# Two layers of convolution and SwiGLU on one core: the same instructions, every engine's queue in a newly searched order

## The chip, the core and the metric

The kernel runs on one core of a Trainium2 chip. The metric is the device time of one execution in microseconds; the time of a kernel is the median of its runs. An execution that the hardware profiler followed gives a trace beside the times: every instruction with its engine, start, duration and what it waited for.

## The reference

`reference(q, k, v, shift_k, ssm_k, ssm_D, x, w_gate, w_up, w_down)` applies two identical layers to x = q, in bf16, with batch 1, S = 2048 rows, D = 512 columns and F = 1792 hidden columns:

```python
def _A_ref(q, k, v, shift_k, ssm_k, ssm_D):
    k_shift = sum over t of k_pad[:, t:t + S, :] * shift_k[:, ks - 1 - t]      # 4 taps, causal
    kv = k_shift * v
    y = irfft(rfft(kv, 2 * S) * rfft(ssm_k, 2 * S))[:, :S]                     # long causal convolution per column
    return q * (y + kv * ssm_D)

def _B_ref(x, w_gate, w_up, w_down):
    return (silu(x @ w_gate) * (x @ w_up)) @ w_down

for _ in range(2):
    x = x + _A_ref(_layernorm(x), A_k, A_v, A_shift_k, A_ssm_k, A_ssm_D)
    x = x + _B_ref(_layernorm(x), B_w_gate, B_w_up, B_w_down)
```

`_layernorm` takes mean and variance over the 512 columns. The convolution's y doesn't depend on x, so the same y serves both layers.

## The kernel before

**The convolution.** k, v and the filter are cut into 4 blocks. The four-tap shift is done on TensorE: `dg` holds diagonal matrices made from the taps (L1372 on ScalarE, L1376 on VectorE, some on GpSimd), and a matmul of `dg` with k, transposed to `kTb`, gives shifted k in PSUM. k is transposed by TensorE for the first block and by SP's transposing DMAs (L460) for the later ones. The transforms are matmuls with cosine and sine blocks of 128x128. The forward ones, `fwd`, are computed at the start in two halves: angles on VectorE (L1324, L1328), Sin on ScalarE (L1330), negations on VectorE (L1336). The inverse ones, `inv`, are two transposing DMAs of `fwd` on SP (L1382). H and G are spectra of the filter, X those of kv; `product` multiplies them on VectorE (t, then Z: L748, L752), `m` is a sum or difference of Z (L889), and the inverse matmuls (L895) give y in PSUM.

**The prologue of a unit.** Work goes by units (layer, c, h) of 256 rows: layer 0 or 1, column of four rows c = 0 to 3, half h. For each, `apply_norm` makes n = layernorm(x), `prologue` forms x += n*y (L1004 to L1009), takes the second layernorm to z, and transposes z to `zT`: by SP's transposing DMA (L994), or on TensorE for the first unit (L1022). Statistics come in two ways: `ln_stats` on VectorE (L914, L915), and `ln_stats_act` on ScalarE (sums L929, mean L931, squares L938, variance `ve` L942). Both end in `power` (L905), an exponentiation on GpSimd that gives `rstd`. `shift_of` (L953) multiplies it with the mean on VectorE for those n that ScalarE normalises (L959).

**The feed-forward part of a unit.** Hidden columns go in groups of 4, 4, 4 and 2 tiles of 128. `pf` are gate and up products (L416, with zT), `sg` is silu of the gate, `ht` or `hr` the other factor, and `pd` the down products (L1210). In groups that `by_rows` makes, the hidden values come with rows on the partitions, so SP transposes them: `sg<-hr` (L1132). Five units use a product of seven instead of eight matrix blocks (L1085).

**What sets the order.** The functions above don't issue anything; they register 1716 operations with a planner (`Plan.add`), each with its engine, its cost, what it reads and writes, and a function that emits it. `ORDER` has one number for each operation, its rank, and `Plan.order` sorts by it. `walk` then goes through the sorted list once and assigns ring slots (PSUM banks and shared SBUF buffers); `issue` emits the instructions in that list's order under a manual schedule, so that each engine's queue, and SP's DMA queue, has the operations in the table's order. An engine runs its queue strictly in order. Ahead of the first real matmuls stand 33 warm-up matmuls (L1495).

```python
def order(self, table):
    assert len(table) == len(self.ops)
    seq = [o for _, o in sorted(zip(table, self.ops), key=lambda x: x[0])]
```

`bst` is a buffer of six slots for the statistics of VectorE; two memsets on GpSimd (L1276, L1277) fill its constant columns.

Of the kernel before, what the change touches and what calls it, by code (L numbers as in the profile page):

```python
# [343 lines left out]
def kernel(  # L344
# [79 lines left out]
    bst = whole("bst", [P, BN_SLOTS, 9], F32)  # L424
# [484 lines left out]
    def ln_stats(c, rows, pw=PW):  # L909
        n = len(rows)  # L910
        mv = new("mv", "mv", [P, n, 2], F32, parts=n)
        for o, i in enumerate(rows):
            st = plan.buf("bn", "bnst", lambda slot: bst.t[:, slot])
# [615 lines left out]
```

## Time and profile before

| | |
|---|---|
| time, median of 3 runs | 339.26 us (339.04 to 339.29) |
| profiled execution, first to last instruction | 337.7 us |
| TensorE busy | 330.9 us, 98% |
| VectorE busy | 299.9 us, 89% |
| ScalarE busy | 262.8 us, 78% |
| GpSimd busy | 35.4 us, 10% |
| granted TensorE clock | 1.000 |
| moved by DMA | 31.59 MB |

In the views of the profile PE is TensorE, PEld its weight loads, DVE VectorE, ACT ScalarE, POOL GpSimd, and SPq the DMA queue that SP issues. A row of the chain has its start and its length in microseconds, the engine, what was made, the line, and how many instructions it groups. A row of the timeline has start, length, engine, line, operation, what was made from what, the tile shapes and the count; in brackets stand the idle time before it and what ended that. A row of the waits has the time waited in all, how often, and the longest. A row of the windows has the stretch, its length, busy times of PE, PEld, DVE, ACT and POOL with their counts, the granted clock, the share that the DMA engines were busy, and GB/s. A duration on PE includes the pipelining with its neighbours.

### The profile page before, as it was taken

The numbers are of one execution on the slowest core, as the hardware profiler recorded it, in microseconds if no ns is written. First come the engines' busy times: TensorE is split into PE (matmuls) and PEld (weight loads), VectorE is DVE, ScalarE is ACT, GpSimd is POOL, SyncE is SP. The second block draws the span as 40 slices with busy tenths as digits, with TensorE's granted clock in tenths as the row PEclk, the third lists the DMA queues.
The fourth block names the chain that finished last, engine by engine and source line by source line (L and its number), as shares of the span: only waits on it lengthen the run. The fifth ranks groups of instructions, "written<-read, shape, count | busy, mean of one in ns | idle before, by whom it ended". The sixth has DMA issues, their size and how long they took to land.

```text
span 337.7 us, 5898 instructions
## 1 busy us (share of the span) xinstructions
PE 330.9 (98%) x2141; PEld 204.6 (61%) x2172; DVE 299.9 (89%) x512; ACT 262.8 (78%) x534; POOL 35.4 (10%) x48
## 2 busy tenths in 40 slices
PE   9999999999999999999999999999999999999996
PEld 7655864645445564745454464744455687858884
DVE  8899999999888998999999999999999787877545
ACT  7889999999967466999899894999675556475462
POOL 4050001102100000122010100011100100100000
PEclk9999999999999999999999999999999999999999
DMA  7999604632346147421324434510514230204101
GB/s 255 350 229 376 130 13 66 151 82 41 71 93 94 36 91 188 95 49 32 62 53 106 97 60 110 138 35 16 96 28 82 56 72 17 48 18 93 49 3 62
DMA packets 77993, 31.59 MB, mean 94 GB/s; under 512 B 69766, under 2 KB 75787, under 8 KB 77963
## 3 DMA queue, kind: packets, MB, share of 16 engines
q1 hardware_dynamic: 77808, 31.13, 39.6%
q8 instruction: 17, 0.28, 0.4%
q14 instruction: 14, 0.11, 0.1%
q10 hardware_dynamic: 154, 0.07, 0.1%
HBM read 12.33 MB, written 2.10 MB: 43 GB/s over the span
## 4 chain that ended last, share of the span: by engine, by line
PE 91%; ACT 4%; DMA 2%; issue 1%; DVE 1%; SPq 1%
PE pf L416 56%; PE pd L1210 20%; PE ps L1085 7%; PE ps L416 6%; DMA kTb<-in_A_k_dram 1%; PE wm L1495 1%; DMA sg<-hr 1%; ACT H L525 1%; SPq L1132 1%; ACT ks L620 1%; ACT n L959 0%; ACT jk L929 0%; DVE t L748 0%; ACT ev L525 0%; ACT hr L1124 0%
## 5 line engine op out<-in xcount | busy, mean ns | idle before, releaser
L416 PEld LDWEIGHTS <-zT 128*128 128x128 bf16 x528 | 51.6, 98 | 58.5 <-DMA zT<-z 0.2
L416 PE MATMUL pf<-wg_sb,zT 128*128 128x512 bf16 x255 | 64.3, 379 | 0.5
L416 PE MATMUL pf<-wu_sb,zT 128*128 128x512 bf16 x260 | 64.3, 379 | 0.2
L1210 PE MATMUL pd<-wd_sb,sg 128*128 128x512 bf16 x189 | 48.1, 379 | 0.9 <-DMA sg<-hr 0.3
L1124 ACT CAST hr<-pf 128x512 bf16<-128x512 f32 x66 | 38.4, 593 | 12.4 <-PE pf L416 8.5
L1123 ACT ACTIVATE sg<-pf 128x512 bf16<-128x512 f32 x66 | 38.8, 608 | 11.3 <-PE pf L416 10.2
L416 PE MATMUL pf<-zT,wg_sb 128*128 128x256 bf16 x368 | 46.0, 273 | 0.1
L416 PE MATMUL pf<-zT,wu_sb 128*128 128x256 bf16 x368 | 45.9, 273 | 0.0
L758 DVE TENSOR_TENSOR t<-X,G 128x4096 bf16<-128x4096 bf16 x18 | 40.9, 2284 | 0.1
L416 PEld LDWEIGHTS <-wu_sb 128*128 128x128 bf16 x368 | 36.0, 98 | 8.1
L416 PEld LDWEIGHTS <-wg_sb 128*128 128x128 bf16 x368 | 35.9, 98 | 7.9 <-issue 0.4
L1183 ACT ACTIVATE sg<-pf 128x512 bf16<-128x512 f32 x46 | 27.3, 607 | 10.8 <-PE pf L416 10.8
L1187 ACT CAST ht<-pf 128x512 bf16<-128x512 f32 x46 | 26.8, 595 | 9.8 <-PE pf L416 8.0
L905 POOL TENSOR_TENSOR rstd<-mv,nhalf 128x2 f32<-128x2 f32 x20 | 17.0, 852 | 158.2 <-DVE mv L915 134.7
L1210 PEld LDWEIGHTS <-sg 128*128 128x128 bf16 x200 | 19.5, 98 | 21.7 <-DMA sg<-hr 0.8
L1210 PE MATMUL pd<-wd_sb,ht 128*128 128x512 bf16 (+1 forms) x124 | 29.7, 369 | 0.1
L914 DVE BATCH_NORM_STATS2 bst<-xc 128x6 f32<-128x512 bf16 x40 | 26.5, 683 | 0.5
L905 POOL TENSOR_TENSOR rstd<-ve,nhalf 128x2 f32<-128x2 f32 x12 | 14.6, 1218 | 111.7 <-ACT ve L942 111.7
L1190 DVE TENSOR_TENSOR ht<-ht,sg 128x512 bf16<-128x512 bf16 (+1 forms) x31 | 16.6, 544 | 8.8 <-ACT sg L1183 4.5
L1130 DVE TENSOR_TENSOR hr<-hr,sg 128x1024 bf16<-128x1024 bf16 x27 | 18.4, 682 | 4.2 <-ACT sg L1123 2.0
L1210 PEld LDWEIGHTS <-ht 128*128 128x128 bf16 x126 | 12.3, 98 | 13.1 <-DVE ht L1190 0.3
L525 ACT ACTIVATE X<-ps 128x512 bf16<-128x512 f32 x32 | 18.4, 604 | 1.6 <-PE ps L416 0.9
(143 smaller groups left out, 522.1 us busy)
## 6 DMA issues: line engine op xcount, KB each, us to landing
hn<-in_A_ssm_k_dram SPq DMA_DIRECT2D x4, 512.0 KB, 3.7
vt<-in_A_v_dram SPq DMA_DIRECT2D x4, 512.0 KB, 5.5
xc<-in_A_q_dram SPq DMA_DIRECT2D x4, 512.0 KB, 5.6
out_dram<-xc SPq DMA_DIRECT2D x15, 128.0 KB, 1.9
wg_sb<-in_B_w_gate_dram SPq DMA_DIRECT2D x1, 1792.0 KB
wu_sb<-in_B_w_up_dram SPq DMA_DIRECT2D x1, 1792.0 KB, 8.9
wd_sb<-in_B_w_down_dram SPq DMA_DIRECT2D x1, 1280.0 KB, 12.1
sg<-hr SPq DMA_TRANSPOSE x66, 2.4
```

What stands on the lines that cost most here:

```text
L416: nc.tensor.matmul(o, lhsT=lhsT, rhs=rhs, start=(n == 0), stop=(n == len(terms) - 1))
L525: add("ACT", act(D), lambda: nc.scalar.activation(out=view(), in_=ps.t[:], func=ACT.Copy, scale=scale), r=[ps], w=[(buf, keys)], conv=conv)
L758: dve(8 * D, lambda t=t, part=part: nc.vector.tensor_mul(out=t.t[:], in0=x.t[:, :, part:part + 1, :].to_broadcast((P, R, 2, D)), in1=g.t[: ...
L905: add("POOL", cost, lambda: nc.gpsimd.tensor_tensor(out=rstd.t[:], in0=var(), in1=nhalf.t[:].to_broadcast((P, n)), op=ALU.pow), r=reads + ...
L914: add("DVE", 0.6, lambda st=st, i=i: nc.vector.bn_stats(out=st.t[:, 0:6], in_=xs[c].t[:, i, :]), r=[(xs[c], (i,))], w=[st])
L1085: nc.tensor.matmul(bank.t[:, half_ * C:(half_ + 1) * C], lhsT=lhsT(i), rhs=rhs(i), start=(first and i == 0 and half_ == 0), stop=(last and ...
L1123: add("ACT", act(D), lambda ps=ps, dst=dst, o=o, which=which: nc.scalar.activation(out=rows(dst, o), in_=ps.t[:], func=ACT.Silu) if which ...
L1124: out=rows(dst, o), in_=ps.t[:], func=ACT.Silu) if which == "g" else nc.scalar.copy(out=rows(dst, o), in_=ps.t[:]),
L1130: dve(n * W, lambda: nc.vector.tensor_mul(out=hr.t[:], in0=hr.t[:], in1=sg.t[:]), [sg], [hr], due=(unit, k / pairs, 0.0, "h"))
L1183: add("ACT", act(D), lambda ps=ps, o=o, sg=sg: nc.scalar.activation(out=sg.t[:, o:o + 2, :], in_=ps.t[:], func=ACT.Silu), r=[ps], w=[(sg, ...
L1187: add("ACT", act(D), lambda ps=ps, o=o, ht=ht: nc.scalar.copy(out=ht.t[:, o:o + 2, :], in_=ps.t[:]), r=[ps], w=[(ht, (o // 2,))], due=(uni ...
L1210: nc.tensor.matmul((pds[o] if not cs.start else pds[HP]).t[:, cs], lhsT=ht.tiles(q, o), rhs=wt["d"].t[:, ft, cs], start=(ft == std0 and no ...
```

## The change

`ORDER` is replaced as a whole: all 1716 ranks are new, and come from a new search in which the mean completion times of three engines are part of the objective. In the new order the first use of a statistics slot comes ahead of the memsets that create `bst`, so a small helper creates the buffer on first use. Nothing else differs; the built programs have the same instructions, and the order differs in the queues of TensorE, VectorE, ScalarE, GpSimd and SP. Behind the table the changed kernel's lines are two further down, and behind the helper seven.

```diff
 ORDER = [
-    7, 79, 141, 188, 2, 3, 1, 15, 23, 4, 12, 0, 5, 13, 68, 9, 10, 6, 8, 11, 28, 19, 14, 24, 20, 25, 32, 33, 38, 69, 144, 146, 18, 46, 17, 45, 22, 43,
...
-    1663, 1678, 1691, 1693, 1699, 1703, 1708, 1711, 1712, 1713, 1714, 1710, 1715,
+    3, 110, 0, 119, 4, 2, 1, 16, 15, 5, 6, 23, 24, 29, 30, 9, 8, 10, 7, 11, 25, 12, 39, 13, 14, 41, 43, 53, 56, 33, 34, 35, 31, 54, 32, 52, 28,
...
+    1670, 1643, 1646, 1639, 1656, 1683, 1698, 1707, 1681, 1682, 1650, 1659, 1699, 1700, 1708, 1709, 1710, 1711, 1712, 1713, 1714, 1715,
 ]
...
+    def stat_slot(slot):
+        if bst.t is None:
+            bst.t = bst.make(0)
+        return bst.t[:, slot]
+
     def ln_stats(c, rows, pw=PW):
...
-            st = plan.buf("bn", "bnst", lambda slot: bst.t[:, slot])
+            st = plan.buf("bn", "bnst", stat_slot)
```

What moves where, of the operations that the prediction speaks of: on ScalarE the second square L938 and the variance L942 of the first unit go ahead of two evictions of X, two L1372 and one copy of transposed filter rows go ahead of the second Sin, and the two L959 go ahead of several evictions of H. On VectorE the first unit's L953 goes from behind all products of the first block to behind the first product of its second half, and the two copies of the taps go ahead of the second half of the angles. On TensorE one inverse matmul goes ahead of the first matmul that reads the k transposed by DMA; the gate and up products are permuted within their groups. On SP the order is the same up to the up weights; behind them the two parts of the down weights change places, and later a load of v and a load of the filter go behind two transposes of hidden values.

126 rows, old and new, of the table ORDER are left out of this document.

## The prediction

> **What bounds the kernel now.** I read the page first, then the waits of TensorE, then the chain of work that ended last, and only then the timeline of the first 33 us and of one wait in layer 1.
>
> ```profile
> span 337.7 us, 5898 instructions
> PE 330.9 (98%) x2141; PEld 204.6 (61%) x2172; DVE 299.9 (89%) x512; ACT 262.8 (78%) x534; POOL 35.4 (10%) x48
> PEclk9999999999999999999999999999999999999999
> PE 91%; ACT 4%; DMA 2%; issue 1%; DVE 1%; SPq 1%
> sg<-hr SPq DMA_TRANSPOSE x66, 2.4
> ```
> ```profile
> PE ps L416 <- DMA kTb<-in_A_k_dram: 0.8, 1, 0.8
> ...
> PE pd L1210 <- DMA sg<-hr: 0.3, 1, 0.3
> PE ps L416 <- ACT ks L620: 0.2, 1, 0.2
> ```
> ```profile
> 4.78 1.00 PE pt L583 x16
> 5.78 0.89 PE pt L472 x16
> ...
> 125.07 5.18 PE pd L1210 x24
> ...
> 268.97 3.49 PE pf L416 x32
> ...
> 333.35 1.32 PE pd L1210 x12
> ```
>
> TensorE is busy 98% of the span at the full clock in every slice, and the chain is TensorE for 91%. So I ask how much of its time is not work. The chain prices a matmul: 5.18/24 = 0.2158 us for 512 columns, 3.49/32 = 0.1091 for 256, 0.89/16 = 0.0556 for 128. Counted from the program, which has the same matmuls before and after, there are 978 of 512 columns, 973 of 256, and 217 of 128, 33 of them warm-up that ends at 4.78; four tiny ones make the 2172 that the page's weight loads count. The work after the warm-up is 978 x 0.2158 + 973 x 0.1091 + 184 x 0.0556 = 211.1 + 106.1 + 10.2 = 327.4 us. It starts at 4.78, and the last matmul ends at 333.35 + 1.32 = 334.67: 329.9 us. **Only 2.5 us are waiting.** Another order of the same instructions can gain no more than that, because neither the warm-up nor the last 3 us change: the last 14 operations on TensorE (of the planner's 1716) stand in the same order in both kernels. How much it can lose has no such bound.
>
> The waits name three places, all in the rows above and below: 0.8 us for the k transpose at 22.76, 0.2 us and some issue gaps between 31.27 and 32.88, and 0.3 us at 241.33. Following the chain's starts against the summed work (its steps at these prices) I read them as about 1.0, 0.7 and 0.5 us, which makes up 2.2 of the 2.5.
>
> The profiled execution has a span of 337.7 us against a median of 339.26 for the runs. The 1.56 us between them lie outside the first and last instruction, and I carry them over unchanged: predicted change of the span = predicted change of the time. What a measurement of this kernel can tell from no change is about 0.2%, or 0.68 us.
>
> **The change part by part: the start-up.** Until the first gate/up matmul at 32.88 both orders have the same 84 TensorE steps, so this stretch ends where its longest chain ends. These rows carry it:
>
> ```profile
> 4.54 13.09 SPq L1382 DMA_TRANSPOSE inv<-fwd  x2
> 17.68 2.68 SPq L460 DMA_TRANSPOSE kTb<-in_A_k_dram  x1
> ...
> 29.30 7.83 SPq L460 DMA_TRANSPOSE kTb<-in_A_k_dram  x1
> ```
> ```profile
> L1382 SPq DMA_TRANSPOSE inv<-fwd x2: 5288/6491/7694, 4.5 to 12.3; - x2
> ```
> ```profile
> 3.89 0.63 ACT L1330 ACTIVATE fwd<-ph 128x512 bf16<-128x512 int32 x1 [0.26 <-DVE ph L1328]
> 4.42 0.68 ACT L1372 ACTIVATE dg<-ident,tapF 128x128 bf16<-128x128 bf16 x2
> ```
> ```profile
> 15.64 1.28 DVE L748 TENSOR_TENSOR t<-X,G 128x1024 bf16<-128x1024 bf16 x2
> 16.33 0.60 ACT L525 ACTIVATE X<-ps 128x512 bf16<-128x512 f32 x1 [0.26 <-PE ps L564]
> ...
> 17.69 0.71 ACT L938 ACTIVATE jk<-xc,nm 128x512 bf16<-128x512 bf16 x1
> ...
> 19.76 0.31 ACT L942 ACTIVATE ve<-sm,eps 128x2 f32<-128x2 f32 x1
> ...
> 20.11 0.68 DVE L889 TENSOR_TENSOR m<-Z 128x1024 bf16<-128x1024 bf16 x1
> 20.15 4.36 POOL L905 TENSOR_TENSOR rstd<-ve,nhalf 128x2 f32<-128x2 f32 x1 [13.43 <-ACT ve L942]
> ...
> 22.76 1.08 PE L416 MATMUL ps<-dg,kTb 128*128 128x128 bf16 x16 [0.82 <-DMA kTb<-in_A_k_dram]
> ...
> 23.88 0.59 ACT L620 CAST ks<-ps 128x512 bf16<-128x512 f32 x1 [0.78 <-PE ps L416]
> ...
> 24.55 0.16 DVE L953 TENSOR_TENSOR nmr<-nm,rstd 128x2 f32<-128x2 f32 x1 [0.61 <-POOL rstd L905]
> ...
> 25.32 1.52 ACT L959 ACTIVATE n<-xc,nmr,rstd 128x512 bf16<-128x512 bf16 x2
> ...
> 26.44 0.68 DVE L1004 TENSOR_TENSOR n<-n,ps 128x512 bf16<-128x512 bf16 x1
> ...
> 30.10 0.73 DVE L621 TENSOR_TENSOR vt<-ks,vt 128x512 bf16<-128x512 bf16 x2
> 30.27 0.78 POOL L905 TENSOR_TENSOR rstd<-mv,nhalf 128x2 f32<-128x2 f32 x1 [5.65 <-DVE mv L915]
> ...
> 31.08 0.73 DVE L964 TENSOR_SCALAR z<-xc,mv,rstd 128x512 bf16<-128x512 bf16 x2 [0.25 <-POOL rstd L905]
> ...
> 31.55 0.72 PE L1022 MATMUL ptz<-ident,z 128*128 128x128 bf16 x8
> ...
> 32.88 0.38 PE L416 MATMUL pf<-zT,wg_sb 128*128 128x256 bf16 x2
> ```
>
> The chain is VectorE's: it has work almost without a break up to L1004 at 26.44, then statistics, z at 31.08, its transposes at 31.55, the first pf at 32.88. In that chain VectorE stands once for something that is not work: 0.61 us before L953 at 24.55, for the inverse square root that GpSimd makes in 4.36 us beside a run of VectorE's tensor_tensors. (At 30.27 the same operation took 0.78.)
>
> *The statistics.* After the change the second L938 and L942 stand on ScalarE ahead of the eviction at 16.33, so `ve` is there at about 16.3 instead of 20.07. VectorE then waits for that eviction with its third product, which gives GpSimd a gap of about 0.1 us (my estimate: the two products from 15.64 end at 16.92 in the trace, a little less by their work, and the eviction ends at 16.93). L953 moves from behind all products to about 20.1, and the two L959 (1.52 us) can begin in the 0.78 us in which ScalarE now stands at 23.1. If GpSimd gets in at the gap, the 0.61 goes and costs at most 0.16 us of waiting there: 0.45 saved. L1004 can't use it all. It needs the inverse matmuls, and they stand behind the k transpose's landing: 22.76, plus 3.08 us of matmuls up to the last one it needs (at the prices above), plus about 0.2 for the hand-over, is 26.04 against 26.44. So I take **-0.35 us**; bounds -0.7 (all of the wait between 31 and 33 gone) and +0.5 (below).
>
> *The k transpose.* One inverse matmul (0.22 us) now stands ahead of the first matmul on kTb. The 0.82 us wait becomes 0.6, but the stretch ends with VectorE's chain: nothing by itself.
>
> *Sin and the early copies.* VectorE copies the taps earlier now, and ScalarE's two L1372 and a transposed-h copy stand ahead of the second Sin (L1330). That Sin ended at 4.52; now it follows the copy, which can't start before TensorE's first transposes of 4.78 are through at about 5.1; with some 0.5 for the copy and its own 0.63 I put its end at 6.2 to 6.5, and the first inverse-table transpose on SP with it: some 1.8 us later than 4.54. Queued behind that on SP are the second table, kTb, and every load after it. I cost this at zero, because SP's issue is set by how fast the queues drain and not by when it starts: the same kTb instruction took 2.68 us at 17.68 and 7.83 at 29.30. Bounds: 0 and the whole 1.8 less the 0.6 of slack, +1.2. On TensorE and VectorE the late Sin shifts the spectra of h; stepping through the first 13 operations by these durations I find TensorE 0.1 us behind where it was, inside the later wait of 0.8. The error of that stepping is some 0.3, hence the +0.5.
>
> **The rest, 33 to 335 us.** The wait in layer 1:
>
> ```profile
> 234.07 5.13 SPq L1132 DMA_TRANSPOSE sg<-hr  x4
> ...
> 241.33 1.04 PE L1210 MATMUL pd<-wd_sb,sg 128*128 128x512 bf16 x4 [0.33 <-DMA sg<-hr]
> ```
> ```profile
> 237.94 3.35 DMA sg<-hr
> ```
> ```profile
> 40.00:60.00 20.00, 19.89 (x122) 11.85 (x122) 19.86 (x29) 19.73 (x42) 1.74 (x2) 1.00 0.23 36
> ```
>
> One transpose took 3.35 us where the median of 66 is 2.4, and TensorE stood for it. The transposes and their users keep their places in the queues there, but the first user comes about 0.86 us earlier, at 236.3, while the first of the four, issued at 234.07, lands at 236.5 by the median: the wait may split, not vanish. From -0.5 to +0.2; I take **-0.1**. Elsewhere VectorE and ScalarE run at 19.86 and 19.73 of 20 us (40 to 60) and TensorE loses 0.11, so there is nothing to gain and something to lose. Comparing the two orders by the matmul work that stands ahead of each transpose's first user, I count 24 users within 1 us of the landing after, 26 before; most of the time they neither wait nor gain. I take **0**, bounds 0 and +1.5 (three further landings of 3.35 us where 2.4 would just do, (3.35 - 2.4) x 3 = 2.85, half of it covered).
>
> Sum: -0.35 - 0.1 + 0 = -0.45, from 339.26 to **338.8 us**, a change inside what can be told from none.
>
> **The rivals.**
>
> *GpSimd shuts VectorE out, or stays shut out (339.2 us).* For: the 4.36 us against 0.78 for the same operation show that the two engines hold each other up. If GpSimd isn't let in at the gap, it runs on beside the products, VectorE stands its 0.6 us at 20.1 instead of 24.55, and L1004 stays at 26.44; if it is let in and VectorE stands for its 0.7 us, the same comes out. Against: at 30.27 GpSimd worked 0.78 us within VectorE's two L621, and VectorE lost nothing. The Trainium skill, "SBUF — State Buffer", section "Who interferes with whom", has a rule that speaks for this rival: a VectorE instruction with two SBUF inputs and a GpSimd instruction that reads SBUF contend for a shared port pair, an exclusive lock, and whichever issues first holds it for the whole instruction. By that rule the early inverse square root only moves the loss; the 4.36 us row agrees with it, the 0.78 us row doesn't show it.
>
> *All three waits shrink (337.9).* The new order places its transposes with the pauses in mind, and half of the 2.5 us goes: 339.26 - 1.3. For: each wait is a single place. Against: only one of them has a mechanism that I can follow.
>
> *The tables come late (340.4; slower).* The mechanism is SP's queue at 4.5 to 23 us. If the time of the table transposes is SP's own and not the queues', a second Sin at 6.3 moves kTb's landing from 22.76 to 24.5, TensorE's 0.6 of wait is used up, and 1.2 us reach L1004, the z transposes and the first pf: 339.26 + 1.2. It decides when kTb is issued later than about 18.3. Against it: the two tables, of one size, took 7.69 and 5.29 us to issue (5288 and 7694 ns in the row above), so 2.4 us of one of them were spent on something other than its size.
>
> *New waits for transposes (340.8; slower).* TensorE's queue is strict, and a pd or pf that reaches the head before its sg or zT has landed stops all behind it. The price is that +1.5 from the bounds above; it decides when three or more of the 24 land over 0.5 us late. For: the 3.35 us row, and ScalarE with 0.27 us of slack in 20. Against: one such wait in 337 us before.
>
> **How the numbers follow.** The forecast 0.42 (its own range 338.2 to 339.5; of it 0.13 below the bound of 338.58, 0.28 within, 0.01 above), GpSimd 0.10, all waits shrink 0.18, tables late 0.12, new waits 0.18. Faster by over 0.2%: 0.13 + 0.18 = 0.31. Within: 0.28 + 0.10 = 0.38. Slower: 0.01 + 0.12 + 0.18 = 0.31. The ceiling of 2.5 us makes anything under 337.8 unlikely, and the two slower cases with their spread reach 341.0.
>
> **What would show it.** Right: the first pf at about 32.5, no VectorE wait before L953 (seven lines further down in the changed kernel), an inverse square root well under 4 us that starts at 16 to 17, and the wait for sg at 241 still there in part. Wrong in the start-up: L953 preceded by 0.6 us at 20; or kTb issued after 18.3 and a first pf after 33.5. Wrong in the rest: the distance from first pf to the last matmul, 334.67 - 32.88 = 301.8 us before, grown or shrunk by over 0.7, with new rows for sg or zT among TensorE's waits.

## The result, and the profile after

The changed kernel takes 338.62 us in the median of 20 runs (338.52 to 339.67), the kernel before, run beside it, 339.55 us (339.04 to 339.96). The ratio is 0.9978 [0.9972, 0.9984]: 0.75 us less, between 0.54 and 0.95. The forecast was 0.45 us less. In the two profiled executions the span went from 337.7 to 337.0 us.

The page after, its head and the shares of the chain:

```profile
span 337.0 us, 5889 instructions
...
PE 331.4 (98%) x2142; PEld 205.0 (61%) x2172; DVE 300.8 (89%) x512; ACT 264.2 (78%) x534; POOL 32.1 (10%) x48
...
PE 94%; DVE 3%; issue 1%; ACT 1%
```

All that TensorE waited for, by the view of its waits:

```profile
PE wm L1502 <- PEq L1520: 0.8, 1, 0.8
```

The kernel before had three more rows there: 0.8 us for the k transpose, 0.3 for `sg` at 241, 0.2 for `ks`. None is left in this execution; the one row that stands is the start of the warm-up, which both kernels have. DMA has gone from the chain, where it had 2%. GpSimd's busy time fell by 3.3 us and no other engine's did; 3.16 of it is one exponentiation, which took 4.36 us and now takes 1.20. The start-up, in the timeline after (lines are two further down, behind the helper seven):

```profile
5.73 0.64 ACT L1337 ACTIVATE fwd<-ph 128x512 bf16<-128x512 int32 x1
...
16.14 1.94 DVE L750 TENSOR_TENSOR t<-X,G 128x1024 bf16<-128x1024 bf16 x3
16.42 0.30 ACT L949 ACTIVATE ve<-sm,eps 128x2 f32<-128x2 f32 x1
...
16.75 0.60 ACT L527 ACTIVATE X<-ps 128x512 bf16<-128x512 f32 x1
16.80 1.20 POOL L907 TENSOR_TENSOR rstd<-ve,nhalf 128x2 f32<-128x2 f32 x1 [9.65 <-ACT ve L949]
...
20.53 0.16 DVE L960 TENSOR_TENSOR nmr<-nm,rstd 128x2 f32<-128x2 f32 x1
...
22.53 1.08 PE L418 MATMUL ps<-dg,kTb 128*128 128x128 bf16 x16
...
24.47 1.90 DVE L891 TENSOR_TENSOR m<-Z 128x1024 bf16<-128x1024 bf16 x3
...
26.29 0.68 DVE L1011 TENSOR_TENSOR n<-n,ps 128x512 bf16<-128x512 bf16 x1
...
30.79 0.73 DVE L971 TENSOR_SCALAR z<-xc,mv,rstd 128x512 bf16<-128x512 bf16 x2 [0.25 <-POOL rstd L907]
...
32.59 0.60 PE L418 MATMUL pf<-zT,wg_sb 128*128 128x256 bf16 x4
```

SP's queue in the same stretch:

```profile
6.39 10.66 SPq L1389 DMA_TRANSPOSE inv<-fwd  x2
17.10 2.34 SPq L462 DMA_TRANSPOSE kTb<-in_A_k_dram  x1
```

The exponentiation starts at 16.80 beside VectorE's three products, and the product with `nmr` stands at 20.53 with no wait in brackets, where 0.61 us stood at 24.55 before. The first n*y comes at 26.29 instead of 26.44, the first `pf` at 32.59 instead of 32.88. The place in layer 1, on TensorE:

```profile
236.24 1.04 PE L1217 MATMUL pd<-wd_sb,sg 128*128 128x512 bf16 x4
...
238.91 2.75 PE L1217 MATMUL pd<-wd_sb,sg 128*128 128x512 bf16 x11
```

Eleven down products follow each other from 238.91 without a pause; before, three ended and the next stood 0.33 us. In the chain the last row is the same twelve matmuls, 0.70 us earlier:

```profile
332.65 1.32 PE pd L1217 x12
```

From the first `pf` to the end of the last matmul it was 334.67 - 32.88 = 301.79 us and is 333.97 - 32.59 = 301.38. So **the two profiles put 0.29 us in the start-up and 0.41 us behind it**. The experiments show that this split is an accident of the two executions.

### The profile page after: what moved, and what is told of

Read it like the earlier page. It is cut to its first block, busy times and chain, and to the rows that moved or that the text cites. A ratio compares the mean times of both kernels' runs of the same rounds, so it can differ in the third digit from the quotient of the medians.

```text
span 337.0 us, 5889 instructions
## 1 busy us (share of the span) xinstructions
PE 331.4 (98%) x2142; PEld 205.0 (61%) x2172; DVE 300.8 (89%) x512; ACT 264.2 (78%) x534; POOL 32.1 (10%) x48
## 4 chain that ended last, share of the span: by engine, by line
PE 94%; DVE 3%; issue 1%; ACT 1%
PE pf L418 58%; PE pd L1217 20%; PE ps L1092 7%; PE ps L418 6%; DVE t L750 1%; PE wm L1502 1%; DVE Z L754 1%; PE ps L897 1%; PE pt L585 0%; DVE m L891 0%; PE pt L474 0%; ACT ks L622 0%; DVE vt L632 0%; DVE G L553 0%; DVE G L555 0%
## 5 line engine op out<-in xcount | busy, mean ns | idle before, releaser
L418 PE MATMUL pf<-wu_sb,zT 128*128 128x512 bf16 x256 | 65.4, 379 | 0.4
L907 POOL TENSOR_TENSOR rstd<-ve,nhalf 128x2 f32<-128x2 f32 x12 | 11.5, 960 | 123.9 <-ACT ve L949 123.9
L527 ACT ACTIVATE X<-ps 128x512 bf16<-128x512 f32 x32 | 19.1, 606 | 1.3 <-PE ps L566 0.7
```

Of the source, the lines that this page charges most:

```text
L418: nc.tensor.matmul(o, lhsT=lhsT, rhs=rhs, start=(n == 0), stop=(n == len(terms) - 1))
L527: add("ACT", act(D), lambda: nc.scalar.activation(out=view(), in_=ps.t[:], func=ACT.Copy, scale=scale), r=[ps], w=[(buf, keys)], conv=conv)
L907: add("POOL", cost, lambda: nc.gpsimd.tensor_tensor(out=rstd.t[:], in0=var(), in1=nhalf.t[:].to_broadcast((P, n)), op=ALU.pow), r=reads + ...
```

## The experiments

The theory after the result had two parts. *Statistics*: the start-up gains because the second square and the variance come before VectorE's run of products, so that GpSimd is done long before anyone needs it. *Fetch*: the wait at 241 isn't a matter of order on SP or TensorE. In the trace's packets an 8 KB packet of kind "instruction" on queue q14 runs from 239.09 for 0.82 us, while the transpose that lands late (issued at 237.94) is under way. (Expectations that name packets or the step to the full rate count from 0.24 us later than the timelines do: their 238.85 is 239.09 here.) The DMA view of the kernel before for 238 to 240 us, and then of the kernel after (name, packets, MB, share of the 16 engines):

```profile
q1 hardware_dynamic: 980, 0.24, 78.2%
q14 instruction: 1, 0.01, 2.6%
```
```profile
q1 hardware_dynamic: 778, 0.18, 45.6%
```

After, the packet comes at 274.42, where two `zT` transposes with slack are under way. The rivals: the start-up gains by its *front* (all ahead of VectorE's first product), and the wait at 241 went because of the *order* of the transposes around it.

Orders were mixed with one helper; numbers are places in the order of issue, and 309 (311) is the first down product.

```python
def window(base, other, p, q):     # base, with its operations p..q in other's order
    return base[:p] + sorted(base[p:q], key=other.index) + base[q:]
```

**The start-up alone, and all but the start-up.**

```diff
-ORDER = before                         # start_new
+ORDER = window(before, after, 0, 309)
```
```diff
-ORDER = after                          # start_old
+ORDER = window(after, before, 0, 311)
```

Expected of the first:

> The kernel before, with only its first 309 planned operations (all that stands ahead of the first down product, 0 to about 45 us) put in the order of the changed kernel. Theory A (the gain has two separate places, 0.29 us in the start-up and 0.42 us at 241 us): first pf at 32.6 instead of 32.88, TensorE's wait for sg<-hr at 241 still there, time 0.3 us below the kernel before. Theory B (one cause in the start-up shifts everything behind it against the DMA and so removes the wait at 241 too): wait gone, 0.7 us below.

Expected of the second:

> The changed kernel, with the operations ahead of the first down product put back into the order of before. Theory A: first pf back at 32.9, no wait for sg<-hr at 241, time 0.4 us below the kernel before (0.3 above the changed kernel). Theory B: the wait at 241 comes back too, time equal to the kernel before.

Measured: start_new 339.07 us, 0.9984 [0.9975, 0.9993], that is -0.54 us (-0.85 to -0.24). start_old 339.31 us, 0.9990 [0.9981, 0.9998], -0.34 us (-0.65 to -0.07). Both parts count, and they make up the whole: -0.54 - 0.34 = -0.88 against -0.75. Which is larger these intervals don't say. The signs are those of two separate places: in start_new the first `pf` comes at 32.47, the fourth transpose still lands after 3.12 us, and TensorE's eight down products at 239.71 take 2.17 us where eight take 1.89 without a pause; in start_old the first `pf` is back at 33.42 and that transpose takes 2.50.

**The front alone, and the old front with early statistics.**

```diff
-ORDER = before                         # front_new
+ORDER = window(before, after, 0, 118)  # 118: VectorE's first product
```
```diff
-ORDER = after                          # front_old
+ORDER = window(after, before, 0, 122)  # and the second square still ahead of the third X eviction
```

> The kernel before, with only what stands ahead of VectorE's first product (the taps, the tables, the transposes and spectra of the filter, about 0 to 15 us) in the order of the changed kernel; the statistics of the first unit stay as late as before. In start_old and in pool_before, which have the front of before, TensorE's transposes at 4.6 us ran at half rate until 5.9 and 6.2 us (until 4.7 in the profile of before), and VectorE stood 1.1 to 1.3 us ahead of its first copy. Front theory (the new front gives VectorE and ScalarE other work in that time, and this, not the statistics, is most of the gain in the start-up): first n times y at about 26.6 to 26.8 even though VectorE stands about 0.6 for the inverse square root, time 0.3 to 0.5 us below before. Statistics theory (as predicted: the 0.61 us is the gain): first n times y later than 26.9, the wait of 0.6 at 24 to 25, time within 0.15 us of before.

> The changed kernel, with what stands ahead of VectorE's first product (0 to about 16 us) put back into the order of before, but the second square and the variance still ahead of the evictions of X. It keeps the early statistics and takes back what the new front cost, an idle stretch of VectorE of 1.02 us ahead of G at 10.79 where the kernel before had 0.10. If that idle stretch ate part of the gain: L1011 (the first n times y) at about 26.05 instead of 26.29, first pf at 32.35 to 32.5, time 0.1 to 0.25 us below the changed kernel. If the inverse matmuls behind the k transpose set the end anyway: first pf at 32.6 and the time of the changed kernel.

Measured: front_new 339.69 us, 1.0006 [0.9997, 1.0015], +0.20 us (-0.10 to 0.51): nothing gained. Its timeline still has the old wait, in the old size:

```profile
20.90 4.45 POOL L905 TENSOR_TENSOR rstd<-ve,nhalf 128x2 f32<-128x2 f32 x1 [13.77 <-ACT ve L947]
...
25.39 0.16 DVE L958 TENSOR_TENSOR nmr<-nm,rstd 128x2 f32<-128x2 f32 x1 [0.61 <-POOL rstd L905]
...
27.27 0.68 DVE L1009 TENSOR_TENSOR n<-n,ps 128x512 bf16<-128x512 bf16 x1
```

front_old 339.64 us, 0.9993 [0.9979, 1.0008]. What was expected of it failed. The timeline says why:

```profile
17.81 0.72 POOL L905 TENSOR_TENSOR rstd<-ve,nhalf 128x2 f32<-128x2 f32 x1 [10.99 <-ACT ve L947]
...
18.24 0.69 DVE L748 TENSOR_TENSOR t<-X,G 128x1024 bf16<-128x1024 bf16 x1 [0.75 <-ACT X L525]
...
27.15 0.68 DVE L1009 TENSOR_TENSOR n<-n,ps 128x512 bf16<-128x512 bf16 x1
```

The statistics are early, and the 0.61 is gone, but on ScalarE they stand ahead of the eviction of X, and VectorE waits 0.75 us for that instead. So the new front gains nothing by itself and is still needed. In before ScalarE still evicts two `ev` from 13.31 on and comes to its first square at 14.28, with X waiting at 14.98. In after one of these evictions is done earlier, the first square starts at 13.22, and both are through at 15.45, when the first eviction of X starts.

**The late variance.** The new order, but with `ve`, its exponentiation, the product with the mean and the two normalisations put back late (the normalisations one eviction of H further back than in before); the second square stays early.

```diff
 # ScalarE's queue
-ve<-sm,eps            behind the second eviction X<-ps
+ve<-sm,eps            behind the fifth
-n<-xc,nmr,rstd x2     around the second H<-ps
+n<-xc,nmr,rstd x2     behind the fourth
 # VectorE's queue
-nmr<-nm,rstd          ahead of the first m<-Z
+nmr<-nm,rstd          ahead of the second
```

> The changed kernel, with five operations put back where the kernel before has them: the variance of the first unit behind the evictions of X on ScalarE, GpSimd's inverse square root behind it, VectorE's product of mean and inverse square root behind all products of the first block, and the two normalisations that use it. Statistics theory (the wait of 0.61 us is the gain of the start-up; the new front is what makes room for it and gains nothing by itself, as front_new showed): GpSimd takes over 4 us again, VectorE stands 0.6 us ahead of that product at 24 to 25, first n times y at 26.9 instead of 26.29, first pf at about 33.1, time 0.4 to 0.6 us above the changed kernel. If the new order of the products carried part of the gain: less than 0.3 above the changed kernel.

Measured: 338.97 us, 0.9987 [0.9978, 0.9996], -0.44 us, some 0.3 us above the kernel after, where 0.4 to 0.6 was expected. The time went the way that was expected, the mechanism wasn't the one: GpSimd wasn't held up (0.72 us), and what came late was the first normalised n. Why GpSimd got in isn't shown: VectorE has no gap there, its product at 20.19 starts 0.34 us behind the one before it, as the product at 19.51 does in before. So this kernel shows what a late variance costs here by way of the normalisations, not what the exponentiation's 4.36 us cost:

```profile
20.14 0.72 POOL L905 TENSOR_TENSOR rstd<-ve,nhalf 128x2 f32<-128x2 f32 x1 [12.99 <-ACT ve L947]
20.19 0.69 DVE L748 TENSOR_TENSOR t<-X,G 128x1024 bf16<-128x1024 bf16 x1
...
24.57 0.15 DVE L958 TENSOR_TENSOR nmr<-nm,rstd 128x2 f32<-128x2 f32 x1
...
26.96 0.69 DVE L1009 TENSOR_TENSOR n<-n,ps 128x512 bf16<-128x512 bf16 x1 [0.37 <-ACT n L964]
```

**The wait at 241: order or packet.** tail_new gives the kernel before the new order for 231 to 250 us alone. pool_before leaves the order of before and gives GpSimd twelve more instructions at 160 us, memsets of a spare tile, so that its instruction packets fall elsewhere; pool_after does the same to the kernel after, right behind the exponentiation that starts at 237.65.

```diff
-ORDER = before                              # tail_new
+ORDER = window(before, after, 1216, 1288)
```
```diff
+    own = host.emit                         # host: one exponentiation on GpSimd
+    def with_pad():
+        own()
+        for _ in range(12):
+            nc.gpsimd.memset(pad[:], 0.0)
+    host.emit = with_pad
```

> The kernel before, with only the 72 planned operations of about 231 to 250 us in the order of the changed kernel, its matmuls and transposes among them. GpSimd has as many instructions ahead as before, so its code is fetched at about 238.8 again. Fetch theory: the fourth sg<-hr transpose takes over 3 us again, TensorE waits 0.2 to 0.6 us for it, time within 0.2 us of before. Order theory: no wait, 0.4 us below before.

> The kernel before in its own order, with twelve memsets of a spare 128x4 tile added on GpSimd behind one of its exponentiations at about 170 us; nothing reads the tile. Fetch theory: the 8 KB instruction packet that the DMA queue q14 moves at 238.85 us in the kernel before, and at 274.19 in the changed one, is GpSimd's own code; with twelve more instructions ahead it is fetched some 20 to 50 us earlier, the fourth sg<-hr transpose lands in 2.4 us instead of 3.35, TensorE doesn't wait at 241, time 0.4 us below the kernel before; first pf stays at 32.9. Order theory (the wait went because the new order puts more between the transpose and its user): packet or not, the transpose takes over 3 us again and the wait of 0.3 to 0.6 us stays; time within 0.1 of before.

> The changed kernel in its own order, with twelve memsets of a spare tile on GpSimd right behind the exponentiation that begins at 237.42 us, so that its code is fetched at 238 to 239.5 us instead of 274. Fetch theory: the fourth sg<-hr transpose, issued at about 237.6, takes over 3 us instead of 2.4, and TensorE waits for it again, 0.2 to 0.5 us; time 0.2 to 0.5 above the changed kernel. Order theory: the landing is late but covered, time as the changed kernel.

Measured: tail_new 339.51 us, 1.0002 [0.9993, 1.0012]: the new order of that stretch gives nothing. The DMA view for 238 to 240 us has the packet still in it (first fence), and the fourth transpose lands after 3.13 us. No row of TensorE's waits names it, but the down products that took 2.75 us in after take 2.95 here (second fence):

```profile
q14 instruction: 1, 0.01, 1.9%
```
```profile
239.46 2.95 PE L1215 MATMUL pd<-wd_sb,sg 128*128 128x512 bf16 x11
```

pool_before 339.39 us, 0.9990 [0.9981, 0.9999], -0.34 us. From 238 to 240 us its DMA view shows only the transposes (first fence); the packet has gone to 160 to 162 (second), and no wait is left at 241, with the old order unchanged:

```profile
q1 hardware_dynamic: 647, 0.15, 36.9%
```
```profile
q14 instruction: 1, 0.01, 1.9%
```

But at 219 to 222 us two such packets meet. They do so in before too, where q14's takes 0.32 us and the transpose of `sg` across them lands after 4.32 without a loss on TensorE; here q14's takes 1.74 (first fence), the transpose lands after 4.72, and the eight down products that need it take 2.09 us where before they took 1.89 (second fence, pool_before and then before):

```profile
q14 instruction: 1, 0.01, 3.6%
q8 instruction: 1, 0.02, 2.0%
```
```profile
222.06 2.09 PE L1210 MATMUL pd<-wd_sb,sg 128*128 128x512 bf16 x8
221.39 1.89 PE L1210 MATMUL pd<-wd_sb,sg 128*128 128x512 bf16 x8
```

The wait moved rather than vanished: from first `pf` to the last matmul this execution took 301.58 us. pool_after 338.95 us, 0.9983 [0.9974, 0.9992], -0.58 us: it has lost 0.17 of the 0.75 (the intervals of the two overlap), the packet is back at 238.85, the fourth transpose takes 3.11 us, and TensorE waits again:

```profile
PE pd L1215 <- DMA sg<-hr: 0.2, 1, 0.2
```

**The two kernels once more**, unchanged, one execution each, to see how far one profile can be trusted.

> The kernel before, unchanged, for a second profile. If the half-rate stretch of TensorE ends at another moment in each execution, its first gate and up matmul comes later than 32.88 by about 0.4 us for each us that the stretch ends after 4.66; otherwise at 32.9 again.

> The changed kernel, unchanged, for a second profile: no wait of VectorE ahead of the product of mean and inverse square root, no wait of TensorE for sg, first n times y at 26.0 to 26.4, last matmul 0.7 to 1.0 us earlier than in the second profile of the kernel before.

Measured: before_again 339.51 us with a span of 337.7, after_again 338.69 with 336.9. after_again went as expected (last matmul 0.86 us earlier), but for a wait of 0.2 us for a `zT` that ScalarE evicts, ahead of the first `pf`. before_again did not: full rate begins at 4.87, as in before, and the first `pf` still comes 0.32 us later; TensorE waits 0.2 us there for the load of k. Set beside the other ten profiled executions (us; starts from the timelines, "middle" is from the first product to the first n*y):

| execution | first product | first n*y | middle | first pf | first pf to last matmul's end |
|---|---|---|---|---|---|
| before | 15.64 | 26.44 | 10.80 | 32.88 | 301.78 |
| before_again | 16.08 | 26.89 | 10.81 | 33.20 | 301.49 |
| tail_new | 16.02 | 26.84 | 10.82 | 33.14 | 301.56 |
| front_new | 16.46 | 27.27 | 10.81 | 33.58 | 301.54 |
| pool_before | 16.45 | 27.25 | 10.80 | 33.55 | 301.58 |
| start_old | 16.30 | 27.11 | 10.81 | 33.42 | 301.37 |
| front_old | 16.21 | 27.15 | 10.94 | 33.45 | 301.38 |
| stat_late | 16.40 | 26.96 | 10.56 | 33.29 | 301.37 |
| after | 16.14 | 26.29 | 10.15 | 32.59 | 301.37 |
| after_again | 15.99 | 26.14 | 10.15 | 32.45 | 301.38 |
| start_new | 16.02 | 26.17 | 10.15 | 32.47 | 301.71 |
| pool_after | 16.20 | 26.34 | 10.14 | 32.65 | 301.54 |

The middle is the same to 0.02 us in every execution that has the same order there, 10.81 or 10.15, which makes the statistics worth **0.66 us**. The first product moves by 0.8 us from one execution to the next whatever the order: the old front has a mean of 16.12 us (six), the new one 16.20 (six). The profiled execution of the kernel before happened to have the earliest of all, so half a microsecond of the gain is hidden in the pair of profiles; 0.14 of it comes back between the first n*y and the first `pf`, which is 6.44 us in before and 6.30 to 6.33 in all others. The last column, from the trace's unrounded times, has two levels. Five executions of the new order behind the start-up, without the packet at 238 to 240, have 301.37 or 301.38; the six with it have 301.49 to 301.78. The fourth transpose takes 3.05 to 3.35 us in those six and 2.48 to 2.52 in the other six. The packet's place is therefore worth 0.11 to 0.41 us, 0.16 in the mean of the four lowest and 0.23 in that of all six (0.15 of start_new's 0.34 is lost at 47.2 instead, where TensorE stands for VectorE's `ht`). Together that is 0.66 + 0.16 or 0.23 = 0.8 to 0.9, against a measured 0.75 (0.54 to 0.95).

Two sums close less well. By the table pool_before should be at the time of before, and was measured 0.34 us under it (0.03 to 0.65); start_old should gain 0.16 and gained 0.34, with 0.16 still inside its 0.07 to 0.65. A front that moves by 0.8 us between executions may be behind it, but that wasn't shown.

## Why the prediction was right, and where it was not

The median of 338.62 lies 0.2 us from the forecast of 338.8, in its own range. The gain of 0.75 us is on the far side of the 0.68 that was said to be the least that can be told, so the case that came true is "faster", if barely (the interval, 0.54 to 0.95, holds both); the forecast's centre lay within the bound. Both terms of the sum were too small, and that the time still lies in the range is owed to the range's 1.3 us.

*The statistics: right mechanism, term of the sum too small (0.35, measured 0.66).* The exponentiation starts at 16.80 within the foretold 16 to 17 and takes 1.20 us, the wait ahead of `nmr` is gone at 20.53, and from its first product to n*y VectorE stood 0.04 us in all, where it stood 0.65. The failed step is the cap "L1004 can't use it all", which held the inverse matmuls behind the k transpose at 22.76. That was read off the one execution with the early front. In the five others that have the old order there, no row names the k transpose, and TensorE waits 0.5 to 0.9 us for VectorE's `m` instead; the view of TensorE's waits of before_again:

```profile
PE ps L895 <- DVE m L889: 0.7, 1, 0.7
```

With a front 0.4 us later, VectorE is the last to come and its 0.61 us count in full. Whether the cap would hold in the new order with a front as early as 15.64, no run shows.

*Sin and the tables: right, at zero.* Sin ended at 5.73 + 0.64 = 6.37 (foretold: 6.2 to 6.5), and the first table was issued at 6.39, 1.85 us later than before. The two tables then took 10.66 us instead of 13.09, and kTb was issued at 17.10 instead of 17.68. In the other executions the tables were issued at 4.7 to 5.1 with the old front and at 6.3 to 6.6 with the new one, and kTb at 15.98 to 16.84 and at 15.99 to 17.58: little of the later start is passed on. This refutes the rival "the tables come late" (340.4), whose sign was a kTb issued after 18.3. What is left open is 0.35 us on the front itself: the earliest first product of the new front is at 15.99 (after_again), that of the old one at 15.64 (before). Two single executions don't tell that from chance.

*The wait at 241: right sign, wrong reason, and small (0.1; 0.41 in the pair, 0.11 to 0.19 in most).* The prediction blamed nothing for the 3.35 us landing and let the users' order move the wait. tail_new shows that the order is worth nothing, pool_before and pool_after that the packet is worth something. That the new order moves this packet to 274 us was luck for the forecast, which knew of no packet. The DMA view of that stretch would have shown the q14 row; I read the chain and the timeline of TensorE there, but not that view.

*The rest from 33 to 335 us: right, at zero.* 301.37 to 301.38 us in five profiles, and no row for a transposing DMA among TensorE's waits of after and after_again: "new waits for transposes" (340.8) is refuted. So is *GpSimd shuts VectorE out* (339.2): GpSimd got in, and VectorE didn't stand. The Trainium skill, "SBUF — State Buffer", section "Who interferes with whom", says that the port pair the two engines share is an exclusive lock. The 4.36 to 4.45 us beside unbroken products, the 0.72 us in a gap of VectorE (front_old) and the 1.20 us after agree that GpSimd waits for its turn; the 0.72 us beside unbroken products in stat_late doesn't fit that, and its cause is open. That VectorE loses as much, which the rival made of it, no row here shows. *All three waits shrink* (337.9) had the right list and the wrong price: the waits in the view of TensorE are all gone, but in a chain that VectorE sets the start-up's were worth 0.66 together, and all of them 0.75, not 1.3.

*The ceiling of 2.5 us* held, and so did the last matmuls: 1.32 us in both.

## What to carry to other kernels

Where one profile gives a cap of a few tenths on a gain, ask which engine would be last if the stretch ahead of it began half a microsecond later; take a second profile of the same kernel before believing the order of two arrivals. A wait for a transfer that took longer than its siblings is looked up in the DMA view of that stretch first: here an instruction packet was in it, and more instructions on GpSimd moved the wait (in pool_before onto another transpose), while a new order of that stretch didn't. An early statistic on an engine that also evicts is worth something only if the evictions ahead of it were moved too.

## What the runs showed of the hardware that was not expected

**The start of the full rate moves from execution to execution.** The warm-up and the first transposes on TensorE run at 0.107 us for 128 columns and then, from one matmul to the next, at 0.056. In the trace that step is at 4.89 us in before, 5.00 in after_again, 5.75 in after and 6.49 in pool_before; in tail_new it is at 4.22. So most of the first 16 transposes in after run at 0.107 us, where the forecast priced them at 0.0556. The chain of pool_before, whose order there is that of before, beside that of after_again:

```profile
4.79 1.80 PE pt L583 x16
```
```profile
4.79 1.04 PE pt L585 x16
```

The same 16 transposes took 1.00 us in before and 1.80 here, and VectorE got its first `hs` 0.8 us later, as the timelines of before and pool_before show:

```profile
5.82 0.42 DVE L599 COPY hs<-pt 128x512 bf16<-128x512 bf16 x1 [0.48 <-PE pt L583]
```
```profile
6.63 0.42 DVE L599 COPY hs<-pt 128x512 bf16<-128x512 bf16 x1 [1.28 <-PE pt L583]
```

The column of the granted clock shows none of it. The windows from 5 to 6 us of before, and of pool_before, have 1.00 there, with 21 and 13 matmuls:

```profile
5.00:6.00 1.00, 1.00 (x21) 1.00 (x20) 0.52 (x3) 0.51 (x2) 1.00 (x2) 1.00 0.59 225
```
```profile
5.00:6.00 1.00, 1.00 (x13) 1.00 (x11) 0.35 (x2) 0.10 (x1) 1.00 (x2) 1.00 0.92 299
```

The Trainium skill, "TensorE: Matmul & The Clock Gate", section "Part 1: The HAM clock gate (the "warmup" mystery)", gives 107 and 56 ns and a change about 4 us into sustained work, 500 ns to either side. The two rates agree. The spread doesn't: counted from the first warm-up matmul at 0.78 the change came after 3.4 to 5.7 us. With the old front and no row of a load among TensorE's waits, a step at 4.89, 6.02 (front_old), 6.11 (start_old) and 6.49 us goes with a first product at 15.64, 16.21, 16.30 and 16.45. The other thing that moved the front is the loads: in front_new TensorE stood 0.4 us for k, in tail_new 0.2 for k and 0.2 for the filter, in before_again 0.2 for k, in before for neither.

**An instruction packet can delay a transpose.** An `sg` transpose takes 2.4 us in the median; the fourth one at 238 us takes 3.05 to 3.35 with a q14 packet across it, and one with two packets at 218 us 3.05 to 4.72. It need not: the transpose at 185.4 us in front_new took 2.42 with a packet across it. That q14 brings GpSimd's code is shown so far as twelve more instructions on GpSimd moved its packet, off 241 in the one kernel and back to it in the other; which engine q8 feeds was not tried.
